# First tile's feed-forward in two halves of 128 rows, unit 3 turned on TensorE, and a new order: block-sparse attention with a channel mix on one core

## The chip, the core and the metric

The kernel runs on one core of one Trainium2 chip. A core has five engines that each work through a queue of their own in order: TensorE (PE; its weight loads are shown apart as PEld), VectorE (DVE), ScalarE (ACT), GpSimd (POOL) and SyncE (SP, which here only issues DMAs). Sixteen DMA engines move data between HBM and the on-chip memory. The metric is the device time of one execution in microseconds; the time given for a kernel is the median of its runs.

## What is computed

Four sequences of 768 tokens, eight heads of 64. First a block-sparse attention in blocks of 32: each query block sees itself and its neighbours, the first and the last block, and three drawn blocks; the first and the last query block see everything. Its output, 512 wide, goes through a channel mix with a feed-forward product.

```python
mask = np.abs(blk_i - blk_j) <= window
mask = mask | (blk_i == 0) | (blk_j == 0) | (blk_i == n_blocks - 1) | (blk_j == n_blocks - 1)
for qb in range(n_blocks):
    for kb in sampled_blocks[qb]:
        mask[qb * block:(qb + 1) * block, kb * block:(kb + 1) * block] = True
scores = np.where(mask, scale * np.matmul(q, k.transpose(0, 1, 3, 2)), -1000000000.0)
attn = np.exp(scores - np.max(scores, axis=-1, keepdims=True))
x = np.matmul(attn / (np.sum(attn, axis=-1, keepdims=True) + 1e-09), v)   # then (B, S, H * D)
...
x_prev = np.concatenate([np.zeros((B, 1, D)), x[:, :-1, :]], axis=1)
xk = mu_k * x + (1.0 - mu_k) * x_prev
xr = mu_r * x + (1.0 - mu_r) * x_prev
k = np.maximum(xk @ w_k, 0.0)          # 512 -> 1024
v = k * k @ w_v                        # 1024 -> 512
r = 1.0 / (1.0 + np.exp(-(xr @ w_r)))  # 512 -> 512
return r * v
```

## The kernel before

**Units.** The attention is cut into 26 units, counted from 0. Units 0 to 21 are query blocks 1 to 22 of all four sequences (128 rows); units 22 to 25 are one sequence each, with its first and last block ("wide"). A unit's keys and values come by DMA; the drawn blocks' places are read out of a packed list on SyncE. Per unit TensorE makes the scores (64 matmuls of 64x32 weights with 256 columns), VectorE the row maxima (`top`), ScalarE the exponentials. The probabilities must then be transposed for the product with the values. There are two ways: units 0 to 2 (`at < MOVE_FROM`) are turned on TensorE, 16 matmuls against the identity into PSUM (`turn`, L368), and copied out by ScalarE or VectorE (L372, L373); from unit 3 on VectorE transposes in 32x32 squares (`near_turn`, L452) and four DMAs of 256 KB put the squares in place (`near_move`, L460). The product with the values takes 128 matmuls of 128x32 weights and 65 columns (L472). `finish` divides and writes the 128 rows of x, transposed, into a tile `xt`.

**Tiles.** The channel mix works on 12 tiles of 256 rows (two query blocks: tile 1 is blocks 2 and 3, that is units 1 and 2, with the last row of unit 0 for `x_prev`), in the order 1 to 10, 0, 11. `split_x` mixes x and x_prev, per chunk of 128 channels one ScalarE scaling (`now`, L663) and one VectorE multiply-add (`mix`, L666), and splits the result into two parts of a shortened float type, a high one (`hi`) and the rest (`lo`). All three weight matrices are split the same way at the start (20 loads of 512 KB, `weight`). Each product is then three matmuls (high by high, high by low, low by high). Per tile: `gate` (L706) makes r in two halves of 128 rows, 12 matmuls of 512 columns each; `hidden` (L726) makes k in four groups of 24 matmuls with 256 columns, the columns being the tile's 256 rows; relu, square and the split of the square follow (L739 to L747); `values` (L759) makes v, 24 matmuls of 512 columns for each half; VectorE multiplies by the gate, SyncE stores.

**Order.** Every step is an operation with a name, an engine and a planned cost in ns in a list (`plan.add`). `choose` picks among several engines by a table `CHOICE`. The list is then issued in an order written out by hand as numbers (`ORDER`, 2,106 of them), so that each engine's queue, SyncE's DMA issues too, follows that list. The planned costs are not used when the kernel runs; what they say is what the layout was made with. TensorE's queue in the old list goes, after the scores of unit 4: both parts of the first gate of tile 1, unit 3's values, three hidden groups with unit 5's scores between them, the rest of the hidden products, unit 4's values, the second gate, unit 6's scores.

## Time and profile before

| what | value |
|---|---|
| median of 3 runs | 519.46 us (518.55 to 524.22) |
| the profiled execution | 523.59 us, of which the span from first to last instruction is 521.8 us |
| mean granted TensorE clock | 0.984 of full speed |
| DMA | 115.68 MB, mean 222 GB/s |

The profile lists, for each engine, busy time and idle time and what ended the idle time. A busy TensorE is not TensorE at its peak: matmuls overlap, and their ends are modelled. What an operation costs in TensorE's queue is therefore read from the spacing of starts, or from the pieces of the chain of waits, not from the mean duration of one matmul. The clock is the share of full speed that was granted; it knows two levels, 1.2 and 2.4 GHz, so a mean of 0.71 over a stretch is a mix of the two.

### The profile page before, as it was taken

To read this page: it belongs to the slowest core of one execution; us is meant where nothing else is said; L and a number is where in the kernel's file an instruction comes from. 1 tells how busy PE (TensorE), PEld (TensorE's weight loads), DVE (VectorE), ACT (ScalarE), POOL (GpSimd) and SP (SyncE) were. 2 spreads that over 40 slices of the span, in tenths; PEclk is the share of its full clock that TensorE was granted. 3 is DMA by queue.
4 is the path that set the end of the run, shared out by engine and by line. 5 is a ranking of instruction groups with operands and counts; after the bars stand their busy time and mean duration, and the time that the engine had idled before them with its cause. 6 is when DMAs were issued, how large, how long until landed. Compare 5 with 4: busy or idle time off the path is not lost.

```text
span 521.8 us, 17723 instructions
## 1 busy us (share of the span) xinstructions
PE 481.7 (92%) x7250; PEld 396.1 (76%) x7250; DVE 349.0 (67%) x675; ACT 304.4 (58%) x695; POOL 129.8 (25%) x147
## 2 busy tenths in 40 slices
PE   0667899899999999999999999989999999999997
PEld 0344578579779788878878888868778879889896
DVE  4687998576876876776876877764867555534351
ACT  3576988575835574646665845653655555455241
POOL 2542434232300601312302201002112320422230
PEclk9997799999999999999999999998999999999999
DMA  8999999978977988888898889999659644000001
GB/s 279 398 357 341 318 309 308 296 209 239 298 228 221 276 230 248 224 273 238 219 282 235 237 260 279 257 266 344 183 136 287 198 116 132 21 21 1 21 21 60
DMA packets 58627, 115.68 MB, mean 222 GB/s; under 512 B 7729, under 2 KB 20785, under 8 KB 55602
## 3 DMA queue, kind: packets, MB, share of 16 engines
q1 hardware_dynamic: 58546, 114.55, 72.2%
q8 instruction: 57, 0.93, 0.7%
q14 instruction: 24, 0.20, 0.1%
HBM read 77.82 MB, written 6.29 MB: 161 GB/s over the span
## 4 chain that ended last, share of the span: by engine, by line
PE 66%; SPq 11%; DMA 9%; ACT 6%; DVE 4%; issue 4%; POOL 0%; DVEq 0%; ACTq 0%; POOLq 0%
PE v L759 18%; PE s L399 6%; PE h_3p L726 6%; PE r_1p L706 5%; PE h_2p L726 5%; PE h_1p L726 5%; PE r_0p L706 5%; PE h_0p L726 5%; SPq L460 5%; PE o L472 4%; DMA KA<-kt 4%; PE o L535 2%; PE sw L493 2%; SPq L578 2%; DMA xm<-rx 1%
## 5 line engine op out<-in xcount | busy, mean ns | idle before, releaser
L759 PE MATMUL v<-w,k 128*128 128x512 f32 (+1 forms) x600 | 141.2, 388 | 1.5 <-ACT xt L615 1.5
L759 PEld LDWEIGHTS v<-w,k 128*128 128x128 f32 x600 | 108.1, 188 | 30.6 <-issue 4.0
L399 PE MATMUL s<-KA,q 64*32 64x256 f32 x1408 | 49.8, 408 | 21.4 <-DMA KA<-kt 17.9
L449 ACT ACTIVATE p<-s,nm 128x256 f32<-128x256 f32 x152 | 63.5, 478 | 0.6
L409 DVE TENSOR_REDUCE nm<-s 128x4 f32<-128x1024 f32 x44 | 53.2, 1217 | 11.2 <-PE s L399 11.0
L399 PEld LDWEIGHTS s<-KA,q 64*32 64x32 f32 x1408 | 27.8, 112 | 36.2 <-issue 25.0
L452 DVE STREAM_TRANSPOSE r<-p 128x1024 f32<-128x1024 f32 x38 | 46.2, 1231 | 5.7 <-ACT p L449 4.8
L472 PEld LDWEIGHTS o<-VA,pt 128*32 128x32 f32 x2432 | 36.0, 109 | 7.8 <-issue 4.4
L472 PE MATMUL o<-VA,pt 128*32 128x65 f32 x2432 | 39.9, 221 | 1.5 <-DMA pt<-r 1.4
L726 PEld LDWEIGHTS h_0p<-xk,w 128*128 128x128 f32 x288 | 36.6, 195 | 2.2 <-issue 1.0
L666 DVE SCALAR_TENSOR_TENSOR xr_1f<-xt,mk,xr_1d 128x128 f32<-128x128 f32 x48 | 17.8, 371 | 30.4 <-ACT xr_1d L663 28.1
L726 PE MATMUL h_0p<-xk,w 128*128 128x256 f32 x288 | 37.8, 286 | 0.0
L726 PE MATMUL h_2p<-xk,w 128*128 128x256 f32 x288 | 37.4, 284 | 0.2 <-ACT h_0k L739 0.2
L726 PE MATMUL h_3p<-xk,w 128*128 128x256 f32 x288 | 37.3, 284 | 0.1
L706 PE MATMUL r_0p<-w,xr 128*128 128x512 f32 x144 | 37.2, 406 | 0.0
L726 PEld LDWEIGHTS h_3p<-xk,w 128*128 128x128 f32 x288 | 35.3, 190 | 2.3 <-issue 0.8
L726 PEld LDWEIGHTS h_2p<-xk,w 128*128 128x128 f32 x288 | 35.4, 190 | 1.6 <-ACT h_0k L739 0.6
L706 PE MATMUL r_1p<-w,xr 128*128 128x512 f32 x144 | 36.5, 399 | 0.0
L726 PE MATMUL h_1p<-xk,w 128*128 128x256 f32 x288 | 36.4, 282 | 0.0
L726 PEld LDWEIGHTS h_1p<-xk,w 128*128 128x128 f32 x288 | 35.1, 189 | 1.3 <-issue 0.8
L706 PEld LDWEIGHTS r_0p<-w,xr 128*128 128x128 f32 x144 | 27.2, 194 | 7.2 <-issue 1.2
L666 DVE SCALAR_TENSOR_TENSOR xr_0f<-xt,mk,xr_0d 128x128 f32<-128x128 f32 x48 | 17.9, 374 | 19.1 <-ACT xr_0d L663 13.7
(202 smaller groups left out, 757.4 us busy)
## 6 DMA issues: line engine op xcount, KB each, us to landing
VA<-vt SPq DMA_DIRECT2D x92, 260.0 KB, 4.6
KA<-kt SPq DMA_DIRECT2D x89, 256.0 KB, 4.5
pt<-r SPq DMA_DIRECT2D x76, 256.0 KB, 5.3
VA<-vw SPq DMA_DIRECT2D x24, 260.0 KB, 5.1
KA<-kq SPq DMA_DIRECT2D x16, 384.0 KB, 5.0
ptw<-rw SPq DMA_DIRECT2D x32, 192.0 KB, 4.1
out<-z SPq DMA_DIRECT2D x23, 256.0 KB, 4.2
q<-qt SPq DMA_DIRECT2D x22, 256.0 KB, 5.1
```

Of the source, the lines that this page charges most:

```text
L399: nc.tensor.matmul(s.ap[ROWS[j], row, a * 256 : (a + 1) * 256].rearrange("p (n x) -> p n x", x=BLK), q.ap[half, (hp * QB + j) * BLK : (hp ...
L409: nc.vector.tensor_reduce(out=nm.ap.rearrange("p (r a) -> p r a", r=2), in_=s.ap.rearrange("p r (a x) -> p r a x", a=2), axis=AX.X, op=ALU ...
L449: plan.add(f"u{name} exp {i}", ACT, 365, lambda row=row, a=a, i=i: nc.scalar.activation(squares()[:, :, :, i, :], s.ap[:, row, a * 256 : ( ...
L452: plan.add(f"u{name} turn", DVE, N_TURN, lambda: nc.vector.transpose(out=r.ap[:, :, gi].rearrange("p j c i x -> p j (c i x)"), in_=squares ...
L460: nc.sync.dma_start(pt.ap[:, b].rearrange("p g c i x -> p (g c i x)"), r.ap[ROWS[b]].rearrange("p j g c i x -> p j (g c i x)"))
L472: nc.tensor.matmul(o[gi].ap[ROWS[j], i * DV : (i + 1) * DV], pt.ap[:, j, gi, g, 2 * row + a, :], VA.ap[:, c0 + g, j, h * DV : (h + 1) * DV ...
L493: nc.tensor.matmul(s.ap[HALF[a], row, 0:W], q.ap[half, 2 * hp * BLK : 2 * (hp + 1) * BLK], wide_keys(b, hp)[half, k * W : (k + 1) * W], st ...
L535: nc.tensor.matmul(o.ap[ROWS[2 * a + e], c * DV : (c + 1) * DV], pt.ap[:, 2 * a + e, row, n, :], VA.ap[:, c1, part, h * DV : (h + 1) * DV] ...
L666: nc.vector.scalar_tensor_tensor(out=parts(f.ap[:, i, :]), in0=cols(c, 1), scalar=mk.ap[:, 2 + which, c : c + 1], in1=parts(d.ap), op0=ALU ...
L706: nc.tensor.matmul(pr.ap[:, 0:512], xr.ap[:, a, c, :], weight_of["r", c].ap[:, w, :], start=(c == 0 and m == 0), stop=(c == CC - 1 and m = ...
L726: nc.tensor.matmul(ph.ap[:, ff * TT : (ff + 1) * TT], weight_of["k", c, f2 // 2].ap[:, w, f % 4 * P : (f % 4 + 1) * P], xk.ap[:, a, c, :], ...
L759: nc.tensor.matmul(pv.ap[:, 0:width], k2.ap[:, a, f, i * P : (i + 1) * P], weight_of["v", f].ap[:, w, cs], start=(f == 0 and m == 0), stop ...
```

## The change

Seven things are changed.

1. The first tile's x (for k) is split in two halves of 128 rows instead of one of 256, and its hidden products are made per half by a new `half_hidden`: four groups (two halves of rows by two halves of the hidden width), each of four operations of 12 matmuls with 128 columns. Its `values` waits for the parts of its own half alone.
2. The first tile's gate is listed as four operations of 6 matmuls instead of two of 12.
3. `MOVE_FROM` goes from 3 to 4: unit 3 is turned on TensorE.
4. The warm-up becomes 32 matmuls of 64 columns in place of 10 of 512, behind two of unit 0's turns.
5. `mix` may go to GpSimd as two instructions (a scaling and an addition); 62 of 148 mixes do.
6. Planned issue costs of DMAs on SyncE are 410 to 640 ns instead of 560 to 760.
7. `ORDER` (2,135 numbers) and `CHOICE` are new throughout. TensorE's queue now goes, after unit 4's scores: hidden products of the first half (the remaining turns of unit 3, a turn of x and unit 3's values between them), unit 5's scores, the first gate, hidden products of the second half with unit 4's values between them, unit 6's scores, the second gate.

```diff
-    def warm(times, ns):
-        w = buf([P, 512], F32, "m", M_BUFS, f"warm{times}", ps)
+    def warm():
+        w = buf([P, 512], F32, "m", M_BUFS, "warm", ps)
...
-                nc.tensor.matmul(w.ap, one[:, 0:P], one, start=(i == 0), stop=(i == times - 1))
+                nc.tensor.matmul(w.ap[:, 0:wide], one[:, 0:P], one[:, 0:wide], start=(i == 0), stop=(i == times - 1))
...
-        plan.add(f"w{i} load", SP, ISSUE, lambda: nc.sync.dma_start(
+        plan.add(f"w{i} load", SP, 480, lambda: nc.sync.dma_start(
...
-        plan.add(f"u{i} drawn keys", SP, NRAND * FETCH + FIND, fetch_keys, reads=[(packed,)], writes=[(KA, *SLOT(own, own + 1, own + 2))],
+        plan.add(f"u{i} drawn keys", SP, NRAND * 580 + FIND, fetch_keys, reads=[(packed,)], writes=[(KA, *SLOT(own, own + 1, own + 2))],
...
-    def split_x(t, which, i0, many, name):
-        dst = buf([P, 2, CC, many * P], F32R, f"x{which}", 1, name)
+    def split_x(t, which, i0, many, name, whole=None):
+        dst = whole or buf([P, 2, CC, many * P], F32R, f"x{which}", 1, name)
+        at = slice(i0 * P, (i0 + many) * P) if whole else slice(0, many * P)
...
+                def mix_pool(d=d, c=c, i=i, f=f):
+                    nc.gpsimd.tensor_scalar(out=parts(f.ap[:, i, :]), in0=cols(c, 1), scalar1=mk.ap[:, 2 + which, c : c + 1], scalar2=None, op0=ALU.mult)
+                    nc.gpsimd.tensor_tensor(out=f.ap[:, i, :], in0=f.ap[:, i, :], in1=d.ap, op=ALU.add)
...
-                plan.add(f"{name} mix {c}", DVE, 105 + 1.13 * tw, mix, reads=[(d,), (x, *ready), (mk, 2 + which)], writes=[(f, i)], port=105 + 1.13 * tw)
+                choose(f"{name} mix {c}", [
+                    (DVE, 105 + 1.13 * tw, 105 + 1.13 * tw, mix),
+                    (POOL, 460 + 2.85 * tw, 0, mix_pool),
+                ], reads=[(d,), (x, *ready), (mk, 2 + which)], writes=[(f, i)])
...
-        for half in range(2):
-            cs = (2 * half, 2 * half + 1)
-            plan.add(f"{name} {half}", PE, 1400, lambda cs=cs: mm(cs),
-                     reads=[(xr, *SPLIT), *[(weight_of["r", c], 0, 1) for c in cs]], writes=[(pr,)], code=12)
+        each = 1 if first else 2
+        for part in range(CC // each):
+            cs = tuple(range(each * part, each * (part + 1)))
+            plan.add(f"{name} {part}", PE, 700 * each, lambda cs=cs: mm(cs),
+                     reads=[(xr, *SPLIT), *[(weight_of["r", c], 0, 1) for c in cs]], writes=[(pr,)], code=6 * each)
...
+    def half_hidden(name, xk, k2, i, g):
+        ph = bank(f"{name}p", False)
+        kk = buf([P, 2 * TT], F32, "kk", 3, f"{name}k")
+        cols = slice(i * P, (i + 1) * P)
+
+        def mm(ff):
+            for c in range(CC):
+                for m, (w, a) in enumerate(TERMS):
+                    nc.tensor.matmul(ph.ap[:, ff * P : (ff + 1) * P], weight_of["k", c, g].ap[:, w, ff * P : (ff + 1) * P], xk.ap[:, a, c, cols],
+                                     start=(c == 0 and m == 0), stop=(c == CC - 1 and m == 2))
+
+        for ff in range(4):
+            plan.add(f"{name} {ff}", PE, 760, lambda ff=ff: mm(ff),
+                     reads=[(xk, *[(*one, i) for one in SPLIT]), *[(weight_of["k", c, g], 0, 1) for c in range(CC)]], writes=[(ph,)], code=24)
...
-                         reads=[(k2, (0, f // 2), (1, f // 2)), (weight_of["v", f], 0, 1)], writes=[(pv,)], code=6)
+                         reads=[(k2, *[(a, f // 2, i) if t == TILES[0] else (a, f // 2) for a in range(2)]), (weight_of["v", f], 0, 1)], writes=[(pv,)], code=6)
...
-                xk = split_x(t, 0, 0, 2, f"xk{t}")
+                if first:
+                    xk = buf([P, 2, CC, 2 * P], F32R, "x0", 1, f"xk{t}")
+                    split_x(t, 0, 0, 1, f"xk{t}_0", xk)
+                else:
+                    xk = split_x(t, 0, 0, 2, f"xk{t}")
...
-            for f2 in range(FC // 2):
+            if first:
+                for g in range(2):
+                    half_hidden(f"h{t}_0{g}", xk, k2, 0, g)
+                split_x(t, 0, 1, 1, f"xk{t}_1", xk)
+                for g in range(2):
+                    half_hidden(f"h{t}_1{g}", xk, k2, 1, g)
+            for f2 in range(0 if first else FC // 2):
                 hidden(f"h{t}_{f2}", xk, k2, f2, last)
...
-MOVE_FROM = 3
+MOVE_FROM = 4
```

## Rows read from the trace of the kernel before

**Rows 1.** The page's first part: each engine's busy us, share of the span, instructions.

```profile
PE 481.7 (92%) x7250; PEld 396.1 (76%) x7250; DVE 349.0 (67%) x675; ACT 304.4 (58%) x695; POOL 129.8 (25%) x147
```

**Rows 2.** Stretches: length; busy us (count) by engine; granted clock, DMA share, GB/s.

```profile
0.00:60.00 60.00, 31.26 (x716) 19.63 (x722) 43.30 (x84) 38.31 (x86) 25.84 (x34) 0.94 0.93 339
60.00:70.00 10.00, 9.07 (x118) 6.50 (x122) 9.32 (x16) 9.63 (x23) 2.40 (x3) 0.71 0.97 306
70.00:80.00 10.00, 10.00 (x220) 9.03 (x210) 9.85 (x17) 7.92 (x17) 4.19 (x4) 1.00 0.97 320
80.00:90.00 10.00, 9.16 (x183) 8.47 (x182) 7.70 (x19) 8.99 (x24) 5.38 (x6) 1.00 0.96 297
90.00:100.00 10.00, 7.44 (x88) 4.88 (x86) 6.45 (x11) 4.01 (x12) 4.14 (x4) 1.00 0.94 304
100.00:340.00 240.00, 238.01 (x4042) 197.90 (x4043) 177.75 (x346) 148.68 (x353) 47.66 (x52) 1.00 0.86 249
340.00:360.00 20.00, 18.27 (x220) 14.51 (x220) 10.41 (x24) 7.35 (x16) 2.19 (x3) 0.91 0.95 292
360.00:500.00 140.00, 140.00 (x1573) 118.46 (x1572) 78.34 (x153) 73.54 (x161) 32.42 (x39) 1.00 0.41 118
500.00:521.80 21.80, 18.51 (x122) 16.69 (x120) 5.86 (x10) 5.92 (x11) 5.56 (x6) 1.00 0.12 41
```

**Rows 3.** TensorE's timeline, 59 to 104 us: start, us, instructions, idle before and releaser.

```profile
59.93 3.80 PE L399 MATMUL s<-KA,q 64*32 64x256 f32 x64 [1.05 <-ACT xt L611]
...
84.54 0.66 PE L594 MATMUL tx<-ident,x 128*128 128x128 f32 x4 [0.84 <-ACT h_1k L739]
...
93.19 1.93 PE L399 MATMUL s<-KA,q 64*32 64x256 f32 x55 [1.09 <-issue]
...
99.96 3.77 PE L759 MATMUL v<-w,k 128*128 128x512 f32 x15 [1.47 <-ACT xt L615]
```

**Rows 4.** The chain of waits in order of time: start, us, piece.

```profile
107.99 1.89 PE s L399 x64
...
115.65 1.97 PE o L472 x128
118.20 2.84 PE h_1p L726 x24
...
345.53 6.07 DMA KA<-kq
...
409.95 2.79 PE r_1p L706 x12
```

**Rows 5.** TensorE's timeline at 34 us: two sets of four turns of unit 1.

```profile
34.22 0.65 PE L368 MATMUL t1 0 0_452<-ident,p 128*128 128x128 f32 x4
...
34.71 0.60 PE L368 MATMUL t1 1 0_457<-ident,p 128*128 128x128 f32 x4
```

**Rows 6.** Groups by line and shape: count, busy us, mean ns, idle before.

```profile
L452 DVE STREAM_TRANSPOSE r<-p 128x1024 f32<-128x1024 f32 x38 | 46.2, 1231 | 5.7 <-ACT p L449 4.8 <-DMA pt<-r 0.8
...
L666 DVE SCALAR_TENSOR_TENSOR xr_1f<-xt,mk,xr_1d 128x128 f32<-128x128 f32 x48 | 17.8, 371 | 30.4 <-ACT xr_1d L663 28.1 <-POOL xr L675 2.0
...
L675 POOL TENSOR_TENSOR xr<-xr_0f,xr 128x256 fp32r<-128x256 f32 x11 | 8.2, 744 | 40.6 <-ACT xr L678 27.4 <-DMA q<-qt 12.7
...
L679 POOL CAST xr<-xr_0f 128x256 fp32r<-128x256 f32 x12 | 4.8, 399 | 65.8 <-DVE xr_0f L666 65.8
...
L666 DVE SCALAR_TENSOR_TENSOR xk1f<-xt,mk,xk1d 128x256 f32<-128x256 f32 x4 | 1.9, 469 | 0.6 <-ACT xk1d L663 0.6
...
L675 DVE TENSOR_TENSOR xk<-xk1f,xk 128x512 fp32r<-128x512 f32 x1 | 1.8, 1776 | 0.0
...
L373 DVE COPY pt<-t1 0 0_452 128x512 f32<-128x512 f32 x1 | 0.7, 690 | 0.3 <-PE t1 0 0_452 L368 0.3
...
L372 ACT COPY pt<-t1 0 1_470 128x512 f32<-128x512 f32 x1 | 0.6, 588 | 0.5 <-PE t1 0 1_470 L368 0.5
```

**Rows 7.** SyncE's timeline: the four DMAs of unit 3's move.

```profile
60.75 4.26 SPq L460 DMA_DIRECT2D pt<-r  x4
```

More of the change, by code (lines that the diff above doesn't have):

```diff
@@ L116, in choose @@
         engine, ns, port, fn = ways[CHOICE.get(name, 0)]
+        if "codes" in more:
+            more["code"] = more["codes"][CHOICE.get(name, 0)]
         plan.add(name, engine, ns, fn, port=port, ways=[w[:3] for w in ways], **more)
@@ L698, in bank, with gate @@
         return buf(shape, F32, tag, bufs, name, ps)
-    def gate(name, xr, z, last):
+    def gate(name, xr, z, first, last):
         pr = bank(f"{name}p", last)
@@ L720, in hidden, with mm @@
         kk = buf([P, 2 * TT], F32, "kk", 3, f"{name}k")
-        def mm(ff):
+        def mm(ff, cs):
             f = 2 * f2 + ff
-            for c in range(CC):
+            for c in cs:
                 for m, (w, a) in enumerate(TERMS):
@@ L773, in mixer @@
         for place, t in enumerate(TILES):
-            last = place >= LAST
+            first, last = not place, place >= LAST
             if xr is None:
                 xr = split_x(t, 1, 0, 1, f"xr{t}_0")
-                xk = split_x(t, 0, 0, 2, f"xk{t}")
+                if first:
[3 more added lines that the diff above has]
+                    xk = split_x(t, 0, 0, 2, f"xk{t}")
             after = TILES[place + 1] if place + 1 < NTILE else None
@@ L781, in mixer @@
             k2 = buf([P, 2, FC, TT], F32R, "k2", 1, f"k2{t}")
[L782 removed]
+            gate(f"r{t}_0", xr, z[0], first, last)
             xr = split_x(t, 1, 1, 1, f"xr{t}_1")
[L784 removed]
+            if first:
[5 more added lines that the diff above has]
+            for f2 in range(0 if first else FC // 2):
                 hidden(f"h{t}_{f2}", xk, k2, f2, last)
             xk = split_x(after, 0, 0, 2, f"xk{after}") if ahead else None
[L787 removed]
+            gate(f"r{t}_1", xr, z[1], first, last)
             xr = split_x(after, 1, 0, 1, f"xr{after}_0") if ahead else None
@@ L799, in block_sparse_attention_channel_mix @@
              writes=[(mk, 0)], table="exp")
-    warm(WARM, 219)
+    warm()
     mask_setup()
```

42 lines of the change are left out of this document (28 added, 14 removed), and 183 rows, old and new, of tables (CHOICE, ORDER).

## The prediction

> **What bounds the kernel now.** I began with the shares of the engines [rows 1]: TensorE is busy for 481.7 of 521.8 us. A busy TensorE need not run at its peak, so the second view is the one by stretches [rows 2]. From 100 to 340 us it is busy 238.0 of 240 us at full clock, from 360 to 500 us without a gap. There only less TensorE work, or less that is left to do, makes the kernel shorter. It stands or works slowly in two places: up to 100 us (4.3 us idle between 60 and 100, 28.7 before 60, a granted clock of 0.71 from 60 to 70 us), and at 340 to 360 us (1.7 us idle, clock 0.91), where the chain of waits shows a load of wide keys of 6.07 us that the matmuls wait for [rows 4].
>
> Before 100 us three things are tight at once. The DMA engines are 93 to 97% busy. VectorE is busy 26.9 us of the 30 between 60 and 90 us, ScalarE 26.5 [rows 2]. So the early stage is set by loads and by the two elementwise engines together, the rest by TensorE's sum.
>
> I price TensorE's work from pieces of the chain that ran without a wait [rows 4]: a unit's scores 1.89 us, its values 1.97, a gate 2.79, 24 hidden products 2.84 (118 ns each). Four turns of 128 by 128 start 0.49 us after the four before them, so 122 ns each [rows 5].
>
> **The stretch that the change is about.** In the timeline [rows 3] the scores of unit 4 start at 59.93 us, and those of unit 6 end at 93.19 + 1.93 = 95.1. In these 35.2 us TensorE does three scores (5.7), two values (3.9), both gates of tile 1 (5.6), its eight hidden groups (8 x 1.42 = 11.4) and one turn of x (0.5): 27.1 us. So 8.1 us are lost: 2.9 to the clock (10 us at 0.71), 0.84 to the wait at 84.54, and the rest to small ones. From there on TensorE's queue is full apart from one wait of 1.47 us before 99.96 [rows 3].
>
> **Part 1, halves.** The 96 products of 256 columns become 192 of 128. No row shows such a product with these weights. By the pieces, 512 columns take 232 ns and 256 take 118, so a column costs 0.446 ns and 128 columns come out at 61 ns [rows 4]: 192 x 61 = 11.8 us against 11.4, 0.4 more. The other bound is the nearest row with the same 128 by 128 weights and 128 columns, the turn at 122 ns [rows 5]: 23.5 us, 12.1 more. A value below 11.4 is excluded, as the columns are the same and only the instructions double. I take 61 ns: the products' type is that of the 118 ns row, the turns are of the plain f32 type, and the f32 scores need 29.5 ns each with eight side by side, 0.92 ns a column, twice the 0.446.
>
> Here a page speaks against the change. The Trainium skill, "TensorE: Matmul & The Clock Gate", section "Back-to-back issue gap", gives about 81 ns for a sustained pair of weight load and matmul at 128 columns, since both have to pass; by it the halves would be an estimated 15.6 us. The same section gives 131 ns at 512 columns, where this trace has 232 [rows 4], so its figures don't carry over as they stand; no row here shows the 128-column case.
>
> What the halves buy: the first half needs only unit 1's rows (with unit 0's last), not unit 2's, so TensorE has product work right behind unit 4's scores, and the first gate need not come first. The splits of x double in number for this tile: eight mixes of 0.37 us in place of four of 0.47 [rows 6], 1.1 us more on VectorE, and on ScalarE an estimated as much; neither stands in TensorE's queue.
>
> **Part 2, unit 3.** Removed: two stream transposes on VectorE (2 x 1.23 us) [rows 6] and four DMAs of 256 KB, whose issue kept SyncE from 60.75 to 65.0 us [rows 7]. Added: 16 turns on TensorE (4 x 0.49 = 2.0 us, of which half come before unit 4's scores) and four evictions of 0.6 to 0.7 us [rows 6], two on VectorE and two on ScalarE. VectorE gains 1.1 us net, ScalarE loses 1.2, the DMA engines lose 1.05 MB of transfers, which is 3.4 us of their time at 306 GB/s [rows 2].
>
> **Part 3, order and choices.** Up to the keys of unit 6, the new list issues 27.1 MB where the old one issues 29.2: three weights of the value product and the move of unit 3 come later or go, unit 7's drawn keys come earlier (counted from the two lists, a near move as 1.05 MB). The DMA engines have moved 60 x 339 + 10 x 306 + 10 x 320 = 26.6 MB by 80 us [rows 2], so 27.1 MB are there at 81.6 us, ahead of need. Before unit 4's scores 19.8 MB stand instead of 20.3: 1.7 us earlier, at 58.2. With the three weights go their joins and splits, so VectorE's list up to unit 6 is some 6 of 65 us shorter in the planner's figures.
>
> 62 of the 148 mixes of x go to GpSimd as two instructions each. The pair isn't in the trace; a 256-column subtraction there takes 0.74 us, a 256-column cast 0.40 [rows 6]. At 128 columns the pair lies between half of that, 0.57, and all of it, 1.14; I take 0.9, as a fixed part does not halve. That is a price for the pair, and some 19 of the 62 have 256 columns. GpSimd goes from 130 to about 185 us of 522, VectorE loses 62 x 0.37 = 23 us. One subtraction of 512 columns on VectorE took 1.78 us, where a copy of that size took 0.69, beside a GpSimd one [rows 6], so the two engines may also slow each other. On TensorE's path I cost all this at nothing: behind 100 us the queue of products covers it. If the cover is gone, each mix is 0.5 us later, with the single-buffered input of the next behind it. The Trainium skill ("GPSIMD Engine Reference", section "Elementwise — side-by-side cycle accounting") has GpSimd near half of VectorE's speed at a two-input operation; the rows agree in kind, 0.74 us there against 0.47 for a two-input mix of the same 256 columns on VectorE [rows 6].
>
> The warm-up goes from 10 products of 512 columns to 32 of 64, which cost between 1.0 us (the 29.5 ns of a score) and 3.9 (a turn's 122 ns). It lies in front of turns that wait for data; I take no change from it.
>
> **The sum.** From unit 4's to unit 6's scores the new list has 5.7 + 3.9 of scores and values, one gate (2.8), the halves (11.8), two sets of turns (1.0) and two turns of x (1.0): 26.2 us. From 58.2 us, with the same 2.9 of slow clock and half of the other 5.2 lost, unit 6's scores end at 58.2 + 26.2 + 5.5 = 89.9, 5.2 earlier. The second gate, 2.8 us, is left for later: 2.4 gained. At 340 to 360 us, 1.7 of idle time and 1.8 of clock are lost; the new list issues the last two parts of that unit's keys ahead of more of the products, and I take half, 1.7. Together 4.1: 523.6 - 4.1 = 519.5 for the profiled execution, which is itself 4.1 above the median; so 519.5 - 4.1 = 515.4 for the median, about 515.
>
> **The rivals.** (a) The halves are slow: 128-column products at 122 ns. For it: no row shows one. Against: the column price. It gives 11.7 more in a stretch whose end sets all that follows: 527. Break-even is at 61 + 4100/192 = 82 ns. Chance 0.10. The Trainium skill's 81 ns of the section named above would leave just nothing of the gain, 519.
> (b) The early gain isn't there: VectorE and ScalarE, at 26.9 and 26.5 of 30 us, hold the halves' inputs back, unit 6's scores end at 93, and the gate left over eats the 2.1: 520. Chance 0.20.
> (c) More is gained: all the small waits between 60 and 95 us and the whole gap at 340 to 360 go: 2.4 + 2.6 + 3.5 + 1 of the 2 us idle between 100 and 340, 9.5: 510. Chance 0.20.
> (d) GpSimd's mixes come late: ten of the twelve tiles, each 0.5 to 1 us: 520 to 525. The gain is gone when they hold TensorE for 4.1 us in all. Against: behind 100 us TensorE stood for only 2 us in 240 [rows 2]. Chance 0.08.
>
> **The numbers.** My own case has 0.42, between 511 and 519 with 515 as its middle. A change of about 1%, 5.2 us, is what a measurement of this kernel can tell from none: faster means below 514.3. Faster: (c) and two fifths of mine, 0.37; slower: (a) and half of (d), 0.14; the same: 0.49. The range reaches from below (c) to just under (a), 507 to 526.
>
> **What would show it.** Right: unit 4's scores near 58 us, 12 half products in 0.73 to 0.8 us, unit 6's scores ending near 90, no more than 3 us idle from 100 to 340. Wrong: half products above 80 ns; GpSimd named as what TensorE or VectorE waits for behind 100 us; a new gap ahead of the wide units; a lower clock where TensorE starves before 60 us.

## The result: 4 to 8 us slower, and the profile after

The changed kernel takes 526.83 us (median of 20 runs, 520.36 to 533.78), the kernel before, run beside it, 520.80 (20 runs, 518.55 to 524.22). The ratio is 1.0081, 95% interval 1.0052 to 1.0110, and like every ratio and every median from here on it leaves out runs more than 1.5% above the fastest of the same kernel, which gives the changed kernel a median of 525.91; the ratio of the two medians over all runs is 1.0116. Timed again later, the ratio was 1.0156. The forecast was 515, range 507 to 526: wrong in direction, and just outside the range. The profiled execution has a span of 529.1 us against 521.8.

The first part of its page, and its stretches (columns as in [rows 2]):

```profile
PE 487.8 (92%) x7384; PEld 408.5 (77%) x7384; DVE 321.6 (61%) x609; ACT 310.6 (59%) x710; POOL 211.6 (40%) x274
```

```profile
60.00:70.00 10.00, 9.78 (x121) 8.23 (x106) 6.35 (x14) 6.66 (x19) 3.06 (x4) 0.92 0.77 249
70.00:80.00 10.00, 10.00 (x242) 8.85 (x242) 9.93 (x18) 8.24 (x20) 5.62 (x8) 1.00 0.73 199
80.00:90.00 10.00, 10.00 (x193) 9.49 (x191) 7.56 (x17) 7.02 (x18) 6.60 (x7) 1.00 0.94 322
90.00:100.00 10.00, 10.00 (x127) 8.71 (x126) 6.33 (x13) 7.11 (x16) 3.80 (x7) 1.00 0.92 311
100.00:340.00 240.00, 231.98 (x3886) 195.07 (x3885) 164.00 (x310) 147.75 (x351) 93.99 (x124) 0.99 0.83 238
340.00:360.00 20.00, 18.90 (x340) 14.16 (x338) 13.03 (x25) 14.39 (x30) 11.19 (x14) 1.00 0.90 297
360.00:500.00 140.00, 138.97 (x1577) 118.35 (x1574) 69.59 (x133) 72.09 (x157) 51.69 (x67) 1.00 0.48 133
```

Beside [rows 2], TensorE's gaps between 60 and 100 us went from 4.3 to 0.2 us, as they were meant to. But it does 6.1 us more (487.8 against 481.7), and between 100 and 340 us it now stands for 8.0 us in place of 2.0. (The 2.0 are the lowest value of their kind: six profiles of the old order, edited or not, have 2.0 to 5.8 us there, thirteen of the new order 4.8 to 9.3.) TensorE's timeline, where it answers [rows 3], and at the longest wait behind:

```profile
59.19 3.06 PE L402 MATMUL s<-KA,q 64*32 64x256 f32 x64
62.18 2.90 PE L771 MATMUL h_01p<-xk,w 128*128 128x128 f32 x24
64.92 0.62 PE L371 MATMUL t3 0 0_991<-ident,p 128*128 128x128 f32 x4
...
81.79 5.47 PE L771 MATMUL h_11p<-xk,w 128*128 128x128 f32 x48
87.19 2.03 PE L475 MATMUL o<-VA,pt 128*32 128x65 f32 x128
...
95.07 1.96 PE L402 MATMUL s<-KA,q 64*32 64x256 f32 x64
...
267.00 3.19 PE L475 MATMUL o<-VA,pt 128*32 128x65 f32 x120 [2.83 <-DMA VA<-vt]
```

48 half products fill the time from 81.79 to 87.19: 112.5 ns each. Unit 6's scores end at 97.0, where the forecast had 89.9 and the kernel before has 95.1.

The forecast's sum had three parts: the start of unit 4's scores, the stage from there to the end of unit 6's scores, and the tail behind that end. All three can be read again. For the profiled execution it had a span of 517.7 (519.5 less the 1.8 around it), and 529.1 came:

| | before | forecast | after | too long by |
|---|---|---|---|---|
| unit 4's scores start | 59.9 | 58.2 | 59.2 | 1.0 |
| from there to the end of unit 6's scores | 35.2 | 31.7 | 37.8 | 6.1 |
| tail to the end of the span | 426.7 | 427.8 | 432.1 | 4.3 |

The three sum to 11.4 us, the distance of 526.8 from 515.4. That the two agree is luck: both profiled executions happen to lie 4.1 us above the medians used (530.92 over 526.83, 523.59 over the 519.46 of three runs). The experiments ask where the second and the third come from.

### The profile page after: what moved, and what is told of

It reads as the page before. It is cut to its first block, busy times and chain, and to the rows that moved or that the text cites. A ratio compares the mean times of both kernels' runs of the same rounds, so it can differ in the third digit from the quotient of the medians.

```text
span 529.1 us, 18138 instructions
## 1 busy us (share of the span) xinstructions
PE 487.8 (92%) x7384; PEld 408.5 (77%) x7384; DVE 321.6 (61%) x609; ACT 310.6 (59%) x710; POOL 211.6 (40%) x274
## 4 chain that ended last, share of the span: by engine, by line
PE 52%; SPq 15%; DMA 15%; DVE 6%; issue 5%; ACT 4%; POOL 2%; DVEq 0%; POOLq 0%; ACTq 0%
PE v L804 15%; DMA VA<-vt 6%; SPq L463 6%; PE r_0p L718 4%; PE s L402 4%; PE h_0p L739 4%; PE h_2p L739 3%; PE o L475 3%; PE h_3p L739 3%; PE h_1p L739 3%; DMA pt<-r 3%; PE r_1p L718 3%; DMA KA<-kq 2%; PE o L538 2%; DMA KA<-kt 2%
## 5 line engine op out<-in xcount | busy, mean ns | idle before, releaser
L804 PEld LDWEIGHTS v<-w,k 128*128 128x128 f32 x600 | 107.9, 188 | 26.2 <-issue 2.7
L402 PE MATMUL s<-KA,q 64*32 64x256 f32 x1408 | 47.1, 402 | 20.5 <-DMA KA<-kt 17.9
L402 PEld LDWEIGHTS s<-KA,q 64*32 64x32 f32 x1408 | 27.2, 112 | 33.9 <-issue 23.7
L475 PEld LDWEIGHTS o<-VA,pt 128*32 128x32 f32 x2304 | 35.4, 112 | 11.4 <-issue 5.0
L668 ACT ACTIVATE xr_1d<-xt,mk 128x128 f32<-128x128 f32 x48 | 19.2, 400 | 27.4 <-POOL xr_1f L672 14.0
L739 PE MATMUL h_3p<-xk,w 128*128 128x256 f32 x264 | 34.3, 282 | 0.7 <-DVE z L810 0.7
L668 ACT ACTIVATE xr_0d<-xt,mk 128x128 f32<-128x128 f32 x48 | 19.3, 402 | 26.1 <-DVE xr_0f L675 18.2
L739 PE MATMUL h_1p<-xk,w 128*128 128x256 f32 x264 | 34.3, 284 | 0.0
L739 PEld LDWEIGHTS h_3p<-xk,w 128*128 128x128 f32 x264 | 32.6, 188 | 1.8 <-DVE z L810 1.1
L739 PE MATMUL h_2p<-xk,w 128*128 128x256 f32 x264 | 33.8, 282 | 0.2 <-ACT z L727 0.2
L739 PE MATMUL h_0p<-xk,w 128*128 128x256 f32 x264 | 33.8, 283 | 0.0
L739 PEld LDWEIGHTS h_0p<-xk,w 128*128 128x128 f32 x264 | 32.9, 191 | 1.0 <-issue 0.4
L739 PEld LDWEIGHTS h_2p<-xk,w 128*128 128x128 f32 x264 | 32.2, 188 | 1.3 <-ACT z L727 0.7
L718 PEld LDWEIGHTS r_1p<-w,xr 128*128 128x128 f32 x144 | 26.2, 188 | 6.8 <-issue 0.8
```

The costliest lines, as they stand in the source:

```text
L402: nc.tensor.matmul(s.ap[ROWS[j], row, a * 256 : (a + 1) * 256].rearrange("p (n x) -> p n x", x=BLK), q.ap[half, (hp * QB + j) * BLK : (hp ...
L475: nc.tensor.matmul(o[gi].ap[ROWS[j], i * DV : (i + 1) * DV], pt.ap[:, j, gi, g, 2 * row + a, :], VA.ap[:, c0 + g, j, h * DV : (h + 1) * DV ...
L668: nc.scalar.activation(parts(d.ap), cols(c, 0), AF.Copy, scale=mk.ap[:, which, c : c + 1])
L718: nc.tensor.matmul(pr.ap[:, 0:512], xr.ap[:, a, c, :], weight_of["r", c].ap[:, w, :], start=(c == 0 and m == 0), stop=(c == CC - 1 and m = ...
L739: nc.tensor.matmul(ph.ap[:, ff * TT : (ff + 1) * TT], weight_of["k", c, f2 // 2].ap[:, w, f % 4 * P : (f % 4 + 1) * P], xk.ap[:, a, c, :], ...
L804: nc.tensor.matmul(pv.ap[:, 0:width], k2.ap[:, a, f, i * P : (i + 1) * P], weight_of["v", f].ap[:, w, cs], start=(f == 0 and m == 0), stop ...
```

## Experiments

In all of them the median of the kernel before, run beside, lies between 519.8 and 523.3 us; ratios are to it. Orders are shown by the names of their operations.

**The price of a half, alone.** In the kernel before, nothing else changed, each of the first tile's hidden products as two of 128 columns, then as four of 64:

```diff
-            for c in range(CC):
+            wide = TT // 2 if name.startswith("h1_") else TT
+            for n in range(0, TT, wide):
+              for c in range(CC):
```

> The old kernel in its old order; only the first tile's 96 hidden products of 256 columns are each made as two of 128 columns. Theory A (a 128-column product costs about as much as a 256-column one; the changed kernel's trace has 24 of them start over 2.74 us, 114 ns each): TensorE gets 192 x 114 - 96 x 118 = 10.5 us more in a stretch where the old kernel lost 8.1 us to clock and waits, so the time rises by 7 to 11 us, to 528 to 532. Theory B (the price of 61 ns holds where the order is not disturbed, and the loss lies in the new order): no more than 1 us, 520 to 522.

> The same with four products of 64 columns in place of one of 256: 384 products. If a product's cost is set by its 128 by 128 weights, each costs 114 ns again, 44 us in all in place of 11.4, and the time rises by 28 to 34 us. If a column of a short product costs twice what it costs in a long one (114/128 = 0.89 ns), 64 columns cost 57 ns, 22 us in all, and the time rises by 7 to 11 us, as with 128 columns. By the column price that I predicted with, 35 ns or so, it rises by 2 to 4 us.

Two of 128: 531.96 us (three runs), ratio 1.0232 (1.0141 to 1.0323), as theory A had it. Four of 64: 588.76 (two runs), ratio 1.1285 (1.1195 to 1.1374): 67 us more, above all three expectations. TensorE's timeline of the first, then that of the second with its stretch (columns as in [rows 2]):

```profile
69.78 5.58 PE L728 MATMUL h_3p<-xk,w 128*128 128x128 f32 x48
75.19 2.84 PE L728 MATMUL h_2p<-xk,w 128*128 128x128 f32 x24
```

```profile
110.40 20.67 PE L728 MATMUL h_1p<-xk,w 128*128 128x64 f32 x96
130.88 10.43 PE L728 MATMUL h_0p<-xk,w 128*128 128x64 f32 x48
```

```profile
110.00:131.00 21.00, 21.00 (x100) 21.00 (x100) 1.56 (x3) 3.14 (x8) 3.33 (x4) 0.50 0.07 26
```

A product of 128 columns took 5.41 us / 48 = 113 ns, against 118 for one of 256 [rows 4]. One of 64 columns took 20.48 / 96 = 213 ns, at a granted clock of 0.50, the lower of the two levels (1.2 GHz); at that level one of 128 takes 215, as a profile further down shows. In the same kernel there is also a stretch of 64-column products at the full clock, just ahead of one at the low clock:

```profile
72.80:76.00 3.20, 3.20 (x31) 3.20 (x31) 3.13 (x10) 2.26 (x5) 0.45 (x1) 1.00 0.98 350
76.30:79.50 3.20, 3.20 (x17) 3.20 (x17) 2.64 (x5) 1.41 (x4) 0.74 (x1) 0.50 0.93 296
```

By their starts, the products of the first stretch follow each other at 112 ns. So the first expectation had the price right, and the clock, at 0.50 for most of the time, doubled it. Below 256 columns the columns don't set the price, and splitting buys nothing: two halves cost 226 ns where the whole costs 118. The weight loads (PEld, the second busy column) fill the whole 21 us. That they set the price is read from that row, not tried by itself. In the old order 192 products at 113 ns in place of 96 at 118 are 10.4 us more; by the medians 9.8 us came out at the end, by the interval 7 to 17.

**The changed kernel with half of the halves' work.** 6 of 12 products per half operation are left out (the low parts of the first three channel chunks), so the first tile's hidden products are incomplete. That leaves 96 x 113 ns = 10.9 us, near the 11.8 that the forecast had for the complete ones.

```diff
                 for m, (w, a) in enumerate(TERMS):
+                    if c < CC - 1 and m: continue
```

> The changed kernel in its own order; each operation of the first tile's halves makes 6 of its 12 products (for the first three channel chunks the low parts are left out of the hidden product, so its output there is less exact); 6 x 114 = 0.68 us is near the 0.73 us that I predicted for the operation. Theory A: 10.9 us of TensorE's work go, the scores of unit 6 end at 88 to 91 us instead of 97, and the time falls by 5 to 8 us, to 518 to 522. Rival C (the loss comes from the new order behind 100 us, where TensorE stood for 8.0 us instead of 2.0): it falls by no more than 2 us.

The stage came out as forecast: unit 4's scores start at 57.15, unit 6's end at 86.94 + 1.96 = 88.9, 31.8 us where the forecast had 31.7. So the forecast's list of what stands in this stage was right, and one price in it was not. Its 5.5 us for slow clock and waits came out as a sum, with more waiting (4.2 us for 2.6) and less slow clock (1.6 for 2.9); in the second profile of this kind, further down, the clock was 0.64 from 70 to 80 us and the stage took 36.9. This execution took 523.19 us, 7.7 less than the profiled one of the changed kernel, as its timeline promised. But its tail was 432.5 us, no shorter, and the median is 521.86, of two runs only (all four: 520.5 to 531.2), with the kernel before at 522.14 beside it. Even with about the forecast's price the forecast, 5 us under the kernel before, would have been wrong.

**All mixes of x back on VectorE.** The 62 choices undone, the order kept.

```diff
-    "xr1_0 mix 3": 1, "xk1_0 mix 2": 1, ... (62 entries)
```

> The changed kernel in its own order, with all 62 mixes that went to GpSimd back on VectorE. Rival D (GpSimd's mixes are late and hold up x): the time falls by 3 us or more, and the idle time of TensorE between 100 and 340 us falls from 8.0 us. Theory A and rival C (SyncE's order is what makes TensorE wait for values): it stays within 2 us, or rises by some us, since VectorE gets some 23 us of work back.

535.16 us, ratio 1.0238 (1.0157 to 1.0320): in this order GpSimd's mixes help. Rival (d) falls. Part of the 535 has another cause, in its stretches and its timeline (the two of the four runs with a mean clock of 0.99 took 531.9 and 533.0, so it is not the whole):

```profile
60.00:64.00 4.00, 4.00 (x21) 4.00 (x21) 4.00 (x9) 2.15 (x5) 0.73 (x1) 0.53 0.88 319
64.00:68.00 4.00, 4.00 (x21) 4.00 (x20) 0.46 (x2) 1.45 (x4) 0.61 (x1) 0.50 1.01 370
68.00:72.00 4.00, 4.00 (x20) 3.79 (x20) 0.18 (x1) 1.05 (x3) 0.00 (x0) 0.50 0.78 316
```

```profile
65.55 5.36 PE L771 MATMUL h_01p<-xk,w 128*128 128x128 f32 x24
70.71 1.07 PE L371 MATMUL t3 1 0_1045<-ident,p 128*128 128x128 f32 x4
```

TensorE had waited 2.26 us before 59.95; the clock was low from 60 to 80 us, and the half products ran at 5.16 / 24 = 215 ns. From unit 4's to unit 6's scores this execution took 48.3 us in place of 37.8. The same shows in one more profile below (unit 3 moved again: clock 0.50 from 60 to 80 us, 46.0 us).

**The same choices in the kernel before.** 60 of the 62 mixes exist there too; its order is kept.

```diff
-                plan.add(f"{name} mix {c}", DVE, ..., mix, ...)
+                choose(f"{name} mix {c}", [(DVE, ..., mix), (POOL, ..., mix_pool)], ...)
```

> The kernel before with 60 of the mixes given to GpSimd, those that the change gives to it and that the kernel before has too, and its order as it was. Theory (GpSimd's mixes are hidden behind 100 us, and VectorE is not what TensorE waits for there): GpSimd's busy time rises from 130 to about 210 us, VectorE's falls by 20 to 25 us, and the time stays within 2 us of 520.8. Rival (mixes of GpSimd come late, as they take 1.1 us where VectorE's take 0.4 us, in an order that was not laid out for them): TensorE waits for the gate's and the hidden inputs after 100 us, and the time is 525 us or more.

520.95 us (11 runs), ratio 1.0042 (1.0008 to 1.0076), with GpSimd at 207.8 us and VectorE at 329.0: within the 2 us expected. In the old order this part buys nothing.

**Unit 3 on TensorE in the kernel before,** first with the turns where VectorE's stood, behind unit 4's scores; then ahead of them.

```diff
-MOVE_FROM = 3
+MOVE_FROM = 4
-u4 0 scores (PE), u3 0 turn, u3 1 turn (DVE), u3 move (SP)
+u4 0 scores, u3 turn x4 (PE), u3 turned x4 (ACT, DVE)       first run
+u3 turn x4 (PE), u3 turned x4 (ACT, DVE), u4 0 scores       second run
```

> The kernel before with unit 3 turned on TensorE (eight sets of turns) in place of DVE's turns and SyncE's move, its order otherwise as it was. The prediction's step for this part: 2.0 us more of TensorE, 2.5 us less of DVE, 4.3 us less of SyncE's queue, in a stretch where TensorE waits for data: 519 to 521 us against 520.8, no difference. Rival (SyncE's queue is what holds the next units' keys and values): unit 4's scores start 2 to 4 us before 59.9 us, and the time falls to 517 to 518 us.

> The kernel before with unit 3 turned on TensorE, the turns now ahead of unit 4's scores in TensorE's order (in the run before they stood behind them, VectorE's in-order queue waited 6.9 us for them, and SyncE's move of unit 4 waited 12.7 us for VectorE). Theory (Part 2 as such costs nothing, its place did): VectorE does not wait, the move of unit 4 is issued at 75 to 76 us in place of 79.5 us, and the time is 520 to 522 us. Rival (turns on TensorE put PSUM copies and TensorE's order into the path of unit 4): unit 4's scores start at 61 us or later, the hidden products start 3 us or more behind 71.4 us, and the time is 525 us or more.

527.84 us, ratio 1.0151 (1.0118 to 1.0183), and 524.79, ratio 1.0068 (1.0040 to 1.0097). Both theories fall: this part is not free in the old order, even with the turns early. SyncE's waits of the first (line, releaser: us, times, longest), and the stretch:

```profile
SPq L460 <- DVE r L452: 14.4, 2, 12.7
```

```profile
70.00:80.00 10.00, 5.59 (x65) 4.95 (x55) 9.83 (x17) 8.69 (x23) 3.66 (x3) 0.68 0.06 23
```

VectorE's in-order queue stood 6.9 us for TensorE's turns, unit 4's transposes came late behind that, SyncE stood 12.7 us at unit 4's move with every later load behind it, and the DMA engines moved 23 GB/s in those 10 us where the kernel before moved 320 [rows 2]. The early version still has 6.2 us of that wait and a DMA share of 0.50 there. The 4.3 us of SyncE that the move had cost [rows 7] were not saved: SyncE came to the next thing it had to wait for sooner.

**The first tile whole again in the new order,** 96 products of 256 columns at the places of the second halves.

```diff
-                for g in range(2):
-                    half_hidden(f"h{t}_0{g}", xk, k2, 0, g)
...
-            for f2 in range(0 if first else FC // 2):
+            for f2 in range(FC // 2):
```

> The changed kernel with the first tile's hidden products whole again: each of 256 columns, 96 in place of 192, at the places where the second halves stood; everything else (unit 3 turned on TensorE, mixes on GpSimd, the rest of the order) as in the changed kernel. Theory (a product of 128 columns costs 113 ns, one of 256 costs 118 ns, so the halves add 96 x 113 = 10.8 us less 96 x 5 = 0.5 us): TensorE has 10.3 us less to do, unit 6's scores end 3 to 8 us earlier than 97.0 (what the early start of the first halves gave is lost), and the time is 520 to 523 us. Rival (the loss is that of the order behind 100 us, which keeps its waits): unit 6's scores end earlier, and the time stays at 525 to 527 us, with 8 us or more of idle TensorE in 100 to 340 us.

527.30 us, ratio 1.0152 (1.0107 to 1.0196). TensorE does 8.9 us less (478.9), and stands 9.2 us between 60 and 97 us; unit 6's scores end at 97.0 again. 2.9 of the 9.2 are my layout's, a result taken out of PSUM late. The halves cost 10 us of work and fill 9 us that else stand empty, so in the new order their net is near nothing here.

**What holds TensorE behind 100 us.** The chain of waits of the changed kernel (start, us, piece; SPq is SyncE issuing DMAs):

```profile
203.01 0.55 SPq L463
...
205.59 1.27 SPq L463
206.91 4.26 DMA VA<-vt
211.30 2.03 PE o L475 x128
...
256.04 2.65 SPq L463
259.03 1.85 SPq L349
...
262.58 4.37 DMA VA<-vt
267.00 3.19 PE o L475 x119
```

A move (L463, 4 us to issue) stands ahead of values that TensorE waits for. So I changed SyncE's order alone, three times: drawn values ahead of the move at two places; then a unit's own next block of values ahead of its move, for seven units; then unit 12's values and move ahead of unit 10's move of x as well.

```diff
-u12 move, u12 values, u13 drawn values       ...  u15 move, u16 drawn values
+u13 drawn values, u12 move, u12 values       ...  u16 drawn values, u15 move      first run
-uN move, uN values     (N = 10, 11, 12, 15, 16, 17, 19)
+uN values, uN move;  u16 drawn values, u15 move as in the first                  second run
-u10 move x, v2_0_0 store, u12 values, u12 move
+u12 values, u12 move, u10 move x, v2_0_0 store                                   third run
```

> The changed kernel with two edits in SyncE's order alone: the drawn values of unit 13 are issued ahead of unit 12's move, and those of unit 16 ahead of unit 15's move. Theory (the new order puts values behind moves on SyncE's in-order queue, and TensorE waits for them at 201.8, 211.3 and 267.0 us): the waits of 1.06, 1.67 and 2.83 us go, TensorE's idle time in 100 to 340 us falls from 8.0 to about 3 us, and the time from 526.8 to about 522. Rival (the queue is full, so that what is moved back is late in its turn): the idle time stays at 6 to 8 us, only elsewhere, and the time stays at 525 to 527 us.

> The changed kernel with SyncE's order alone edited: a unit's own next block of values (0.6 us to issue) is issued ahead of that unit's move (4.2 us) for the seven units where the new order has it behind (10, 11, 12, 15, 16, 17, 19), and unit 16's drawn values ahead of unit 15's move. Theory (what was late at 211 us was unit 12's own block, issued at 206.9 behind the move of 203.0; the edit of unit 13's drawn values pushed that block to 212.3 and the wait from 1.7 to 4.8 us): the waits of TensorE for values at 211 and 267 us shrink from 4.8 us in all to 0 to 1 us, idle TensorE in 100 to 340 us falls from 8.0 to 3 to 4 us, and the time is 522 to 524 us. Rival (the queue as such is full, or the block of values waits for its place in the ring and holds the move back): other waits of 4 to 6 us stand in their place, and the time stays at 526 to 529 us.

> The mended order itself once more, for times beside the run above and a second profile. Theory: 523 to 525 us; from the start of unit 4's scores to that of unit 6's 35.9 us; behind them 428 to 430 us if TensorE keeps its clock in 200 to 250 us. Rival (that profile was a lucky one): 432 us or more behind the start of unit 6's scores, as without the edit.

> The mended order with one edit more in SyncE's queue: unit 12's own values and its move are issued ahead of unit 10's move of x (3.0 us to issue) and a store. Theory (the wait at 205 to 212 us is that of unit 12's move, issued 3.6 us too late): the waits for moved weights at 205 and 207 us (0.36 and 1.09 us, up to 2.7 in other profiles) go, idle TensorE in 200 to 250 us falls from 3.1 to 1 to 2 us, and the time by 1 to 2 us under that of the mended order in this set. Rival (unit 10's x is then late for its tile): a wait for xt or the gate's input near 225 us in its place, no gain.

> The changed kernel itself once more, for a second profile and times beside the runs of this set. Theory (unit 4's scores start anywhere from 54 to 60 us, by the first 60 us, and behind them the run is fixed: 36 us to the start of unit 6's scores, 434 us from there to the end): the profile has those two stretches within 1 us again, whatever the start, and the median is 526 to 528 us. Rival (the profile taken first was an odd one): the stretch behind unit 6's scores is 430 us or less.

The changed kernel itself, timed once more: 528.85, ratio 1.0156 (1.0112 to 1.0200). First edit: 529.65, 1.0167 (1.0128 to 1.0206). Second edit: 524.47, 1.0060 (1.0034 to 1.0087), and when timed again 529.35, 1.0114 (1.0053 to 1.0176). Third: 528.95, 1.0101 (1.0040 to 1.0161). The intervals of the second edit and of the changed kernel (1.0081 and 1.0156) overlap crosswise, so no gain is shown. TensorE's timelines say why, one fence per kernel: first edit, second, second again, third:

```profile
216.48 3.70 PE L475 MATMUL o<-VA,pt 128*32 128x65 f32 x128 [4.78 <-DMA VA<-vt]
```

```profile
206.91 2.01 PE L475 MATMUL o<-VA,pt 128*32 128x65 f32 x122 [1.09 <-DMA pt<-r]
```

```profile
212.21 3.55 PE L475 MATMUL o<-VA,pt 128*32 128x65 f32 x122 [1.44 <-DMA pt<-r]
```

```profile
209.01 2.93 PE L739 MATMUL h_3p<-xk,w 128*128 128x256 f32 x12 [4.41 <-ACT h_1k L752]
```

What I issued earlier was no longer waited for; what I had pushed back was. First the block of values, then the move, then, in the third, unit 10's move of x: ScalarE's in-order queue stood for it and so emptied a hidden group's place in PSUM late. ScalarE's timeline of the third:

```profile
206.74 0.62 ACT L586 COPY xt<-xm 128x512 f32<-128x512 f32 x1 [7.73 <-DMA xm<-rx]
```

And the work right behind a long wait can run slow: a unit's values products, which take 1.97 us [rows 4], took 3.2 to 3.7 behind three of the waits shown (2.83, 4.78 and 1.44 us), and 2.0 behind the fourth (1.09). The granted clock tells them apart. Stretches of the first edit behind its 4.78 us, and of the changed kernel behind a wait of 1.67 (columns as in [rows 2]):

```profile
216.50:220.10 3.60, 3.60 (x128) 3.42 (x128) 0.00 (x0) 0.00 (x0) 0.00 (x0) 0.50 0.49 128
```

```profile
211.30:213.20 1.90, 1.90 (x128) 1.87 (x128) 0.00 (x0) 1.02 (x3) 0.00 (x0) 1.00 0.86 274
```

The same edit in the kernel before, and in the changed kernel with half of the halves' work, with the halves whole, and with unit 3 moved by SyncE as before:

```diff
-uN move, uN values     (kernel before: N = 7, 11, 12, 15, 19, 20)
+uN values, uN move
```

> The kernel before with the same edit of SyncE's order (a unit's own next block of values ahead of that unit's move, for units 7, 11, 12, 15, 19 and 20, where the old order has it behind). Theory (TensorE waits for no values in 100 to 340 us of the kernel before, its idle time there is 2.0 us in all, so the edit repairs the new order alone): 519 to 521.5 us, no difference. Rival (values ahead of moves are better anywhere): 517 to 518 us.

> The same edit of SyncE's order, in the changed kernel with 6 of 12 products per half operation (the low parts are left out for the first three channel chunks of the first tile's hidden products, 96 products in all), so that TensorE spends about what the prediction had for the halves. Theory (two causes that add: the halves' true price, worth some 5 us at the end, and the order of SyncE's queue, worth some 4 us): 516 to 519 us. Rival (what is gained at 90 us is given back behind 100 us whatever SyncE's order): 522 to 526 us, with 6 us or more of idle TensorE in 100 to 340 us.

> The changed kernel with SyncE's order mended and the first tile's hidden products whole (256 columns, 96 products), at the places of the second halves, their results taken out of PSUM at once. Theory (the halves let TensorE begin at 62 us what it else begins at 73 us, and pay 10.3 us of TensorE for it): from the start of unit 4's scores to that of unit 6's 33 to 35 us in place of 35.9, and a time 1 to 3 us under that of the mended order, 521 to 523 us. Rival (the halves' early start is worth their price): 36 us or more, and 525 us or more.

> The changed kernel with SyncE's order mended, and unit 3 turned by VectorE and moved by SyncE as in the kernel before (two VectorE turns and four more DMAs). Theory (the turns on TensorE cost 3 to 4 us, as in the old order): the time falls to 520 to 522 us. Rival (they cost nothing where the order was laid out for them): the time stays at 524 to 525 us or rises, as SyncE has 4.3 us more to issue at 60 us.

In the kernel before 521.34, ratio 1.0035 (0.9998 to 1.0073): nothing, as expected. Half the work: 522.71, 1.0028 (0.9994 to 1.0062). Whole: 526.77, 1.0138 (1.0087 to 1.0190); from the start of unit 4's scores to that of unit 6's it took 33.9 us, as expected, but its tail 432.5, and its time came out no lower. Unit 3 moved: 525.22, 1.0081 (1.0042 to 1.0120), so in the new order, laid out for them, the turns cost nothing that can be measured.

**Filling the gap ahead of unit 4's scores** with 12 products of 512 columns, output unused:

```diff
+    plan.add("fill", PE, 219 * FILL, run_fill, writes=[(fill,)])
```

> The changed kernel with twelve idle-filling products of 512 columns on TensorE, bf16, their output unused, put ahead of unit 4's scores (2.6 us of work at the full clock, in a place where TensorE waited 2.6 us). Theory (TensorE's granted clock falls when the engine is idle at 54 to 60 us; if it is low when the products of 128 columns begin, it stays low for as long as they run, 17 us in one profile; so runs differ by up to 12 us): the clock is 1.00 from 60 us on, the highest times fall from 534 to about 528 us, and the median from 526.8 to 523 to 525 us. Rival (the clock of this stretch doesn't set the end, as the data is late anyway): the median rises by the filling's own 2 us to 528 or 529 us, with as wide a spread.

532.05 us, ratio 1.0197 (1.0153 to 1.0241). The theory falls, and the rival was too low. The filling itself met a low clock (0.80 from 60 to 70 us) and took 5.1 us in place of 2.6. Unit 4's scores were put off to 64.32 us, and the DMA engines moved 107 GB/s from 60 to 70 us, as SyncE waits 8.0 us for those scores before it may overwrite the keys they read.

**The stretches of all profiles** (us, from TensorE's timelines; stage: start of unit 4's scores to the end of unit 6's; idle: TensorE from 200 to 250 us). In the new order the tail holds the second gate, 2.85 us, which the old order has in the stage.

| kernel | unit 4 starts | stage | tail | idle |
|---|---|---|---|---|
| before | 59.9 | 35.2 | 426.7 | 0.2 |
| before, values ahead of moves | 58.7 | 34.3 | 425.8 | 2.3 |
| before, mixes on GpSimd | 59.6 | 33.0 | 426.5 | 0.8 |
| before, unit 3 turned / turned early | 57.5 / 60.9 | 42.3 / 35.4 | 423.7 / 424.5 | 0.6 / 0.7 |
| before, halves / quarters | 57.8 / 59.0 | 42.9 / 101.2 | 427.1 / 426.9 | 0.3 / 0.5 |
| after / again | 59.2 / 57.7 | 37.8 / 38.9 | 432.1 / 433.4 | 3.6 / 3.1 |
| after, first edit of SyncE's order | 60.0 | 38.6 | 430.5 | 6.4 |
| after, second edit / again | 54.4 / 58.2 | 37.8 / 38.7 | 426.3 / 431.6 | 3.1 / 2.7 |
| after, third edit | 56.0 | 37.8 | 432.2 | 5.2 |
| after, whole / with second edit | 58.2 / 56.4 | 38.8 / 35.9 | 431.7 / 432.5 | 7.1 / 5.5 |
| after, half the work / with second edit | 57.2 / 57.8 | 31.8 / 36.9 | 432.5 / 432.5 | 4.5 / 3.1 |
| after, mixes on VectorE | 55.7 | 48.3 | 431.6 | 4.1 |
| after, unit 3 moved, second edit | 58.9 | 46.0 | 432.0 | 2.7 |
| after, filled | 64.3 | 36.7 | 426.9 | 3.5 |

Less the gate, the tail of the new order is 427.7 to 430.6 us in 11 of 13 profiles, that of the old one 423.7 to 427.1 in all seven. TensorE's wait between 200 and 250 us stands in every profile of the new order (2.7 to 7.1 us; in the old one 0.2 to 0.8, and 2.3 with its queue edited), with halves or whole, with unit 3 turned or moved, with mixes on GpSimd or on VectorE. So it belongs to the order of work itself, not to one of the parts that I could undo. That is an argument by exclusion: each part was undone alone, never all together. Which items of the order bring it is not settled. SyncE issues for 44.5 of these 50 us in the new order and for 43.5 in the old one, so in these two profiles its load hardly differs.

Two things go with a longer tail in the profiles: TensorE's idle time, and the clock behind it. With the idle time, the lost clock (time by the share not granted) and the gate taken off, the tails of the new order lie between 412.0 and 415.6 us and those of the old one between 416.0 and 417.3, so nothing else in the new tail is longer. From 97 to 340 us the granted clock is 1.00 in all old-order profiles except that with quarters, whose scores of unit 6 end at 160 us only; in the new order it is 0.99 in ten of thirteen. The other three are the filled one and the second edit's first, whose tails without the gate are no longer than the old ones (424.1 and 423.5 us, with 4.8 and 5.3 us idle from 100 to 340), and the one with mixes on VectorE (428.7, with 8.6 idle).

## Why the prediction was wrong, step by step

- **Part 1, the price of a half product: mis-sized, 113 ns for 61.** The column price held between 512 and 256 columns [rows 4] and I drew it on to 128; it ends there. 192 x 52 ns are 10.0 us more. They did not all come out in the stage (6.1 too long), because of the 5.5 us allowed for waits and slow clock only 0.2 and 1.2 occurred: 26.2 + 10.0 + 1.4 make 37.6 of the 37.8. With half the work 4.2 us of waits were back, so the longer work had filled them. The row that I set aside, the turn at 122 ns [rows 5], was the right neighbour: same weights, same columns. I chose by the data type and should have chosen by the shape. Rival (a) was this price, and its 527 is what came, though part of it by another way; I had given it a chance of 0.10 and drawn the range to end just under it. The Trainium skill's figure that spoke against the change ("TensorE: Matmul & The Clock Gate", section "Back-to-back issue gap", 81 ns) pointed the right way, and the measured 113 decides. The same page of the Trainium skill, section "LDWEIGHTS (loading the stationary operand)", has a weight load at columns / 1.2, an estimated 107 ns for 128; the full-clock rows come within 6 ns of that, the 215 ns at the low clock do not.
- **The stage around it: right in sum.** With about the forecast's amount of product work it took 31.8 us for 31.7 in one profile, and 36.9 in the other, whose clock was low. Unit 4's scores started 1.0 later than the 58.2 forecast in the profile shown, and between 54.4 and 60.0 in those of the new order without the filler.
- **Part 2, unit 3 on TensorE, costed at nothing on the path: no cost shown in the new order** (moved again: 525.22 against 524.47 and 529.35 with the turns), wrong as a statement about the edit by itself: in the old order it costs 3.6 to 8 us. I counted what VectorE and SyncE save and did not ask what they then wait for.
- **Part 3, mixes on GpSimd, costed at nothing behind 100 us: right, though the pair is dearer than I took.** The groups of line, shape, count, busy us and mean ns:

```profile
L671 POOL TENSOR_SCALAR xr_1f<-xt,mk 128x128 f32<-128x128 f32 x23 | 15.8, 688 | 20.2 <-DVE xr L687 13.2 <-DVE nmw L506 4.6 <-ACT z L727 1.5
...
L672 POOL TENSOR_TENSOR xr_1f<-xr_1f,xr_1d 128x128 f32<-128x128 f32 x23 | 10.6, 460 | 28.5 <-ACT xr_1d L668 25.2 <-ACT xt L589 2.0
```

  At 128 columns 688 + 460 ns, 1.15 us, for the 0.9 taken and the upper bound of 1.14; hence 211.6 us of GpSimd and not 185. TensorE waits for none of them behind 100 us, and undoing them makes the kernel slower.
- **The gap at 340 to 360 us: the number came, but not shown by the change.** 1.7 us idle and a clock of 0.91 [rows 2] became 1.1 and 1.00; 1.7 were to be gained there, and about 2.4 were (0.6 of waiting, 20 x 0.09 = 1.8 of clock). But five other profiles of the old order, each with one edit elsewhere, have 0.0 to 1.3 us idle there and a clock of 1.00, and two of the new order have 2.0 and 2.9 us and 0.91. So the gap belonged to the one profile that I read, and its gain is luck. Rival (b)'s 520 left this gain out; with it that sum gives 518.5, and nothing hangs on it.
- **The tail, costed at nothing: the step that failed beside the price.** I took it that behind 100 us the queue of products covers the new order, because it had covered the old one [rows 2]. But the cover belongs to an order in which each value and move was in time, and the order was new everywhere. 4.3 us of the error are here, and a right price for the halves would not have brought the forecast time: with half their work the changed kernel still took 521.9 (two runs), and 522.7 with SyncE's order edited. I had named "no more than 3 us idle from 100 to 340" as a sign of being right; it was 8.0.

So, shown: the price, its 10.4 us of work, and about 10 us at the end in the old order. Shown too, in one profile for each: the tail's loss stays when any one of the three parts is undone. Not settled: which place in the order, and how much of the halves' price reaches the end in the new one, where the runs with half of it were 4.1 us (521.86, of two runs, against 525.91) and 1.8 to 6.6 us (522.71 against 524.47 and 529.35) under those with all of it. No version here is shown to beat the kernel before.

## What to carry to other kernels

Before splitting a matmul into narrower ones, look for a row with the same weights and the narrow width, even of another type (here 122 ns stood for 113). If there is none, measure one, since a price per column need not hold below the widths the trace has. When a hand-laid order is replaced from end to end, "covered before" is not a price of nothing: sum the in-order DMA queue for the new order, item by item, and give the tail a range. A wait that one edit removes can be back at the next late item, as it was in each of the three edits here. And a forecast read from one profile takes over that profile's chance events: a gap that other profiles of nearly the same kernel do not have need not be there to be gained.

## What the runs showed of the hardware

- With weights of 128 by 128, products of 256 columns took 118 ns, of 128 columns 113 and of 64 columns 112 at full clock; at the low level, products of 128 and of 64 columns took 215 and 213.
- In two profiles the granted clock was 0.50 to 0.53 from 60 us, about where the half products began, and stayed low to 80 us with TensorE busy throughout (4.00 of 4.00 us in each stretch). In a third, the changed kernel timed again, it was 0.70 from 60 to 64 us, with the half products beginning at 61.3, and 1.00 from 64 to 68. In the seven profiles of the new order with complete halves other than those two it was 1.00 from 70 to 100 us. With products of 64 columns it was 0.54 on the mean from 72 to 155 us, with TensorE busy for all 83 us; both levels occur within them, as the two stretches above show.
- Over the 20 runs of the changed kernel the mean granted clock goes from 0.974 (531.6 and 533.8 us) to 0.997 (520.4, 520.5 and 524.6 us); a straight line through the 20 runs makes an estimated 10 of the 13 us of spread go with the clock (correlation -0.84).
- A wait of TensorE can cost more than itself: in nine rows of the new order's profiles a unit's values products behind a wait of 1.4 to 4.8 us took 0.7 to 1.7 us longer than their 2.0 us, and the granted clock over them was 0.50 to 0.70; behind six other waits, of 1.1 to 3.1 us, they did not, and it was 1.00. The length of the wait does not tell which it will be: 1.4 us had the low clock behind it, 3.1 had not.
